# Score products of a pooled attention: one product per head on half of the array's rows, in two banks, in place of pairs of heads with zeros

## The chip, the cores and the metric

One Trainium2 chip, one core. The metric is the device time of one execution in microseconds (us), as the median of several runs. All tensors come from and go to the chip's main memory.

## The reference

Three layers follow each other, for 4 batches x 576 positions = 2304 tokens and 512 channels (8 heads x 64):

```python
k_p = k.reshape(B, H, 72, 8, 64).mean(axis=3)      # 576 keys pooled to 72
v_p = v.reshape(B, H, 72, 8, 64).mean(axis=3)
scores = scale * np.matmul(q, k_p.transpose(0, 1, 3, 2))
scores = scores - np.max(scores, axis=-1, keepdims=True)
attn = np.exp(scores); attn = attn / (np.sum(attn, axis=-1, keepdims=True) + 1e-09)
x = np.matmul(attn, v_p)                           # to (2304, 512)
x = (sigmoid(x @ w_gate) * (x @ w_val)) @ w_out    # 512 -> 1536 -> 512
h = x @ w_in                                       # 512 -> 2048
out = (h * tanh(softplus(h))) @ w2_out             # 2048 -> 512
```

The weights arrive as 64-bit floats and are converted on the chip.

## The kernel before

**Stages.** Tokens are worked on in tiles of 128 (T = 0 to 17). Attention for tiles 0 to 3 runs first; the rest of it is spread through the first three passes of the gated layer (blocks j = 0, 1, 2 of 512 tokens, twelve f each). A pass computes, for each f, `part(pg, ...)` and `part(pv, ...)` (12 products of 512 columns each) and then `emit_out` for the f before. After each of the three comes a `slot`, and a slot runs the words of one section of a schedule written out by hand (`START`, sections parted by `|`). The last 768 tokens of the gated layer and the whole second layer follow after about 340 us and are not touched.

**Order.** Every engine works its instructions strictly in the order in which the words issue them; waits come from the data and from the reuse of buffers. The words that matter: `mT.g` scores of tile T, group g (`att_scores`), `MT.g` the minimum over keys on VectorE (`att_max`; scores carry a minus sign), `XT.g` exp and sum on ScalarE, four heads one by one (`att_exp`; with `:v` partly on VectorE), `NT` the division (`att_norm`), `tT.g` transposes on TensorE, `cT.g` their copy out, `pT.g` or `OT` the products with v. Tiles from 8 on turn the weights by DMA in place of `t`. `A`, `B`, `C`, `G` are steps of weight conversion and splitting. The words around tiles 6 and 7:

```
| | m6.0 C:a M6.0 m6.1 A M6.1 X6.0 X6.1 G:v B:d C:a N6:v | A B:v C:a m7.0 M7.0 X7.0
| t6.0 c6.0:a B:e G:p Q8 | m7.1 M7.1 X7.1 t6.1 c6.1:a B:a N7:v | Q9
| t7.0 c7.0:a t7.1 c7.1:a G:v L2.0 L2.1 | O6 O7 o6 o7 | d m8.0 M8.0 m8.1 M8.1
```

Tile 4 has `m4.0` and `m4.1` in slots some 10 us apart, tile 7 in slots 6.5 us apart; elsewhere the two follow each other with no other TensorE work between.

**Scores.** `q_t[T]` holds q turned, 128 rows = two heads of 64 channels, for four pairs of heads. `kb` holds the pooled keys of a pair as 128 x 144: the even head's 72 columns have zeros in the lower 64 rows, the odd head's in the upper 64. So one product of 128 x 128 weights (q) with 144 columns (`kb`) gives the scores of both heads. Group g covers pairs 2g and 2g + 1, that is heads 4g to 4g + 3, in one bank. A float32 product shows as two records (load of weights and product) in the trace. Tiles 4 and 13 hold tokens of two batches, so each product is done in two parts of 64 tokens.

**Banks.** Scores, transposes and products with v of tiles from 4 on share the tag `at`, two buffers of 128 x 512 float32, taken in turn; a new tile waits until its buffer's last reader is done. q has two buffers as well.

Of the kernel before, what the change touches and what calls it, by code (L numbers as in the profile page):

```python
# [57 lines left out]
def tile_pooled_attention_moe_mish(  # L58
# [12 lines left out]
    nc = tc.nc  # L71
    NT, DM = out.shape
    B, _, NPAIR, S = kt.shape
    SP = S // POOL
    D = DM // (2 * NPAIR)
# [48 lines left out]
    with tc.manual_schedule():  # L124
# [90 lines left out]
        with ExitStack() as actx:  # L215
# [67 lines left out]
            kb = [pt_pool.tile([128, NPAIR, 2 * SP], F32, name=f"kb{i}") for i in range(2)]  # L283
# [95 lines left out]
            def segs(t0, n):  # L379
                done = 0  # L380
                while done < n:
                    b, s = divmod(t0 + done, S)
                    m = min(n - done, S - s)
                    yield done, m, b
                    done += m

            q_t, e_t, mx_t, sm_t, pt_t, sc_t = {}, {}, {}, {}, {}, {}
# [6 lines left out]
            def ps_tile(tag, name):  # L394
                pool = {"mm": ps_mm, "at": ps_at}.get(tag, ps_acc)
                return pool.tile([128, 512], F32, tag=tag, name=name)

            def att_scores(T, g, tag="at"):
                if g == 0:
                    e_t[T] = pt_pool.tile([128, 8, SP], F32, tag="e", name="e", bufs=2)  # L400
                    mx_t[T] = pt_pool.tile([128, 8, 1], F32, tag="mx", name="mx", bufs=2)
                    sm_t[T] = pt_pool.tile([128, 8, 1], F32, tag="sm", name="sm", bufs=2)
                ps = ps_tile(tag, "sc")
                for pp in range(2):
                    for t0, n, b in segs(128 * T, 128):
                        nc.tensor.matmul(
                            ps[t0 : t0 + n, 144 * pp : 144 * pp + 144],
                            q_t[T][:, 2 * g + pp, t0 : t0 + n],
                            kb[b % 2][:, 2 * g + pp, :],
                            start=True,  # L410
                            stop=True,
                        )
                sc_t[T, g] = ps[:, 0:288].rearrange("p (h k) -> p h k", h=4)

            def att_max(T, g):
                mx = mx_t[T][:, 4 * g : 4 * g + 4, :]
                nc.vector.tensor_reduce(out=mx, in_=sc_t[T, g], axis=AX.X, op=ALU.min)  # L417

            def att_exp(T, g, eng=None):
                s = sc_t.pop((T, g))  # L420
                if eng is nc.vector:
                    e, h = e_t[T], slice(4 * g, 4 * g + 4)
                    mx = mx_t[T][:, h, :].to_broadcast([128, 4, SP])
                    eng.tensor_sub(out=e[:, h, :], in0=mx, in1=s)
                    nc.scalar.activation(out=e[:, h, :], in_=e[:, h, :], func=AF.Exp)
                    eng.reduce_sum(out=sm_t[T][:, h, :], in_=e[:, h, :], axis=AX.X)
                    return
                for h in range(4):
                    nc.scalar.activation(  # L429
                        out=e_t[T][:, 4 * g + h, :],  # L430
                        in_=s[:, h, :],
                        func=AF.Exp,
                        scale=-1.0,
                        bias=mx_t[T][:, 4 * g + h, :],
                        accum_out=sm_t[T][:, 4 * g + h, :],
                    )

            def att_norm(T, eng):
# [164 lines left out]
            with tc.tile_pool(name="pst", bufs=1, reuse_waits="tile") as pst:  # L603
# [6 lines left out]
                    out=shift,  # L610
# [73 lines left out]
                def run(word):  # L684
# [11 lines left out]
                    elif op == "V":  # L696
                        att_values(*a, eng)
                    elif op == "m":
                        att_scores(*a, sc_tag[a[0]] if first else "at")
                    elif op == "M":  # L700
                        att_max(*a)
                    elif op == "X":
                        att_exp(*a, eng)
                    elif op == "I":
                        first_loads[a[0]](eng or nc.sync)
# [165 lines left out]
            for j, (o, n) in enumerate(blocks[:-1]):  # L871
# [26 lines left out]
                for f in range(NF):  # L898
# [11 lines left out]
                    if pv is None:  # L910
# [3 lines left out]
                        out=sg, in0=sg, scalar=1.0, in1=pv[:, :n], op0=ALU.add, op1=ALU.mult  # L914
# [71 lines left out]
            for f in range(NF):  # L986
# [52 lines left out]
                g = x1c[:, 2048 + 768 * (f % 2) : 2816 + 768 * (f % 2)].rearrange("p (a n) -> p a n", a=2)  # L1039
# [82 lines left out]
        with ExitStack() as bctx:  # L1122
# [56 lines left out]
            for p in range(NPR):  # L1179
                o = 2 * NG * p  # L1180
                for i in range(NFP):
                    n = NFP * p + i
# [144 lines left out]
```

## Time and profile before

| | us |
|---|---|
| median of 3 runs (lowest, highest) | 874.67 (874.61, 877.69) |
| the profiled execution's own time | 876.79 |
| its span in the trace | 874.7 |
| TensorE busy | 864.3 (99%) |
| VectorE / ScalarE / GpSimd busy | 618.4 / 440.2 / 98.8 |

Times of the trace count from the start of the span. PE is TensorE's products, PEld its loads of weights, DVE VectorE, ACT ScalarE, POOL GpSimd, SP the queue that issues DMAs. Records of products overlap, since each includes its way through the array; the distance between starts tells how long a product holds the array.

### The profile page before, as it was taken

The page shows a single profiled execution, that of the slowest core. Times are in us where ns is not written, and L with a number is a line of the kernel's source. Part 1 is how long each engine was busy: PE and PEld are TensorE (multiplying, and loading weights), DVE is VectorE, ACT ScalarE, POOL GpSimd, SP SyncE. Part 2 cuts the span into 40 slices and gives each one's busy share as a digit, 9 for nine tenths or more (in the row PEclk, how much of TensorE's full clock was granted, in tenths as well). Part 3 has the DMA queues.
Part 4 walks back from the last instruction along what each step waited for, and adds up shares of the span by engine and source line. Part 5 has one row for each costly group of instructions (what it writes and reads, how often), then busy time and mean ns, then how long its engine had stood idle before and what let it go on. Part 6 is the DMA issues. An engine that isn't in the chain of part 4 may idle for free.

```text
span 874.7 us, 12861 instructions
## 1 busy us (share of the span) xinstructions
PE 864.3 (99%) x4628; PEld 768.9 (88%) x4628; DVE 618.4 (71%) x1174; ACT 440.2 (50%) x1052; POOL 98.8 (11%) x110
## 2 busy tenths in 40 slices
PE   8999999999999999999999999999999999999998
PEld 7877888888878888999999999998999988999986
DVE  6879864776755754778898977767677757777632
ACT  6655663554546644534544554445454454445431
POOL 3566430120120000000100000000000000000000
PEclk9999999999999999999999999999999999999999
DMA  7688645998878877155555811202112111110011
GB/s 270 224 295 273 231 154 198 283 266 255 259 184 267 268 212 251 61 217 195 216 197 182 302 53 49 85 25 96 61 49 65 65 40 61 62 47 25 1 37 36
DMA packets 68347, 133.77 MB, mean 153 GB/s; under 512 B 27196, under 2 KB 32060, under 8 KB 68284
## 3 DMA queue, kind: packets, MB, share of 16 engines
q1 hardware_dynamic: 66988, 130.70, 46.0%
q10 hardware_dynamic: 1296, 2.26, 0.7%
q8 instruction: 36, 0.59, 0.3%
q14 instruction: 27, 0.22, 0.1%
HBM read 99.50 MB, written 28.20 MB: 146 GB/s over the span
## 4 chain that ended last, share of the span: by engine, by line
PE 89%; DMA 5%; ACT 3%; DVE 2%; POOL 1%; issue 1%; SPq 0%; POOLq 0%; ACTq 0%; DVEq 0%
PE acc L1156 23%; PE p L122 7%; PE p L120 7%; PE p L121 7%; PE acc L120 4%; PE acc L121 4%; PE acc L122 4%; PE q L120 3%; PE q L122 3%; PE q L121 3%; PE pg L566 3%; PE pv L566 3%; PE pg L567 3%; PE pv L567 3%; PE pg L570 3%; PE pv L570 3%
## 5 line engine op out<-in xcount | busy, mean ns | idle before, releaser
L1156 PE MATMUL acc<-w,g 128*128 128x512 f32 x864 | 201.1, 390 | 0.0
L1156 PEld LDWEIGHTS acc<-w,g 128*128 128x128 f32 x864 | 161.8, 188 | 32.7
L122 PE MATMUL p<-top,w2s 128*128 128x384 f32 x216 | 72.5, 336 | 0.0
L120 PE MATMUL p<-top,w2s 128*128 128x384 f32 x216 | 72.4, 335 | 0.0
L121 PE MATMUL p<-top,w2s 128*128 128x384 f32 x216 | 72.3, 335 | 0.0
L242 ACT ACTIVATE cv<-raw 128x512 f32<-128x512 f32 x66 | 44.9, 681 | 39.8 <-DMA raw<-w2i 14.3
L256 DVE SCALAR_TENSOR_TENSOR cv<-raw,cv 128x512 uint32<-128x512 uint32 x68 | 57.2, 841 | 2.3
L918 ACT CAST gh<-sg 128x512 fp32r<-128x512 f32 x36 | 22.3, 621 | 69.7 <-DVE sg L913 69.7
L120 PE MATMUL acc<-gh,wo 128*128 128x512 f32 x144 | 57.4, 398 | 0.0
L121 PE MATMUL acc<-gl,wo 128*128 128x512 f32 x144 | 56.4, 392 | 0.6 <-DVE gl L766 0.6
L122 PE MATMUL acc<-gh,wo 128*128 128x512 f32 x144 | 56.1, 390 | 0.0
L1150 DVE TENSOR_TENSOR g<-g,g 128x384 fp32r<-128x384 f32 x48 | 26.2, 557 | 31.0 <-ACT g L1146 30.7
L251 DVE TENSOR_SCALAR cv<-cv 128x512 uint32<-128x512 uint32 x68 | 37.2, 546 | 13.1 <-ACT cv L242 13.0
L429 ACT ACTIVATE e<-sc,mx 128x72 f32<-128x72 f32 x140 | 42.5, 326 | 7.2 <-DVE mx L417 7.1
L120 PEld LDWEIGHTS p<-top,w2s 128*128 128x128 f32 x216 | 40.6, 188 | 1.0
L121 PEld LDWEIGHTS p<-top,w2s 128*128 128x128 f32 x216 | 40.5, 188 | 1.0
L122 PEld LDWEIGHTS p<-top,w2s 128*128 128x128 f32 x216 | 40.5, 188 | 0.0
L120 PE MATMUL p<-x1c,w2s 128*128 128x384 f32 x120 | 40.1, 334 | 0.0
L121 PE MATMUL p<-x1c,w2s 128*128 128x384 f32 x120 | 40.1, 334 | 0.0
L122 PE MATMUL p<-x1c,w2s 128*128 128x384 f32 x120 | 40.1, 334 | 0.0
L1212 ACT ACTIVATE g<-g 128x384 f32<-128x384 f32 x24 | 12.6, 527 | 52.4 <-DVE g L1205 52.4
L1146 ACT CAST g<-g 128x384 fp32r<-128x384 f32 x48 | 23.8, 512 | 28.8 <-PE acc L1156 28.8
(261 smaller groups left out, 2153.1 us busy)
## 6 DMA issues: line engine op xcount, KB each, us to landing
wo<-wod SPq DMA_DIRECT2D x39, 512.0 KB
ws<-w2d SPq DMA_DIRECT2D x24, 512.0 KB
raw<-w2i SPq DMA_DIRECT2D x16, 512.0 KB
raw<-w2o SPq DMA_DIRECT2D x16, 512.0 KB
raw<-wv SPq DMA_DIRECT2D x12, 512.0 KB
raw<-wo SPq DMA_DIRECT2D x12, 512.0 KB
wod<-wo SPq DMA_DIRECT2D x12, 512.0 KB
wsd<-ss SPq DMA_DIRECT2D x12, 512.0 KB
```

What stands on the lines that cost most here:

```text
L120: nc.tensor.matmul(ps, wt[:, 0, cols], xh, start=start, stop=False)
L121: nc.tensor.matmul(ps, wt[:, 0, cols], xl, start=False, stop=False)
L122: nc.tensor.matmul(ps, wt[:, 1, cols], xh, start=False, stop=stop)
L242: eng.activation(out=f32(c), in_=hi, func=AF.Prelu, scale=BIAS, alpha=-(2.0**32))
L251: nc.vector.tensor_scalar(out=c, in0=c, scalar1=3, scalar2=None, op0=ALU.logical_shift_left)
L256: nc.vector.scalar_tensor_tensor(out=c, in0=lo, scalar=29, in1=c, op0=ALU.logical_shift_right, op1=ALU.bitwise_or)
L429: nc.scalar.activation(out=e_t[T][:, 4 * g + h, :], in_=s[:, h, :], func=AF.Exp, scale=-1.0, bias=mx_t[T][:, 4 * g + h, :], accum_out=sm_t ...
L566: nc.tensor.matmul(ps[:, c0:c1], w, xh[:, k, c0:c1], start=(k == 0), stop=False)
L567: nc.tensor.matmul(ps[:, c0:c1], w, xl[:, k, c0:c1], start=False, stop=False)
L570: nc.tensor.matmul(ps[:, c0:c1], w, xh[:, k, c0:c1], start=False, stop=(k == KD - 1))
L1150: nc.vector.tensor_sub(out=g[:, 1, :], in0=src, in1=f32(g[:, 0, :]))
L1156: nc.tensor.matmul(acc[t][0], g[:, a, c], w[:, b, :], start=(f == 0 and first), stop=(f == NF2 - 1 and last),)
```

## The change

For tiles from 4 on, `att_scores` with g = 0 takes both buffers of `at` and issues one product per head: the 64 rows of its channels (upper half for even heads, lower half for odd ones), 72 columns of `kb` without the zeros; even heads go to the first bank, odd heads to the second, by turns. With g = 1 it does nothing. `att_max` and `att_exp` of group 0 then cover the even heads, those of group 1 the odd ones. The schedule's words stay.

```diff
+            ROWS = 4
+            def heads(T, g):
+                return slice(g, 8, 2) if T >= ROWS else slice(4 * g, 4 * g + 4)
...
             def att_scores(T, g, tag="at"):
...
+                if T >= ROWS:
+                    if g:
+                        return
+                    ps = [ps_tile(tag, "sc") for _ in range(2)]
+                    for t0, n, b in segs(128 * T, 128):
+                        for h in range(8):
+                            r, c = slice(D * (h % 2), D * (h % 2) + D), SP * (h // 2)
+                            nc.tensor.matmul(
+                                ps[h % 2][t0 : t0 + n, c : c + SP],
+                                q_t[T][r, h // 2, t0 : t0 + n],
+                                kb[b % 2][r, h // 2, SP * (h % 2) : SP * (h % 2) + SP],
+                                start=True,
+                                stop=True,
+                            )
+                    for i in range(2):
+                        sc_t[T, i] = ps[i][:, 0:288].rearrange("p (h k) -> p h k", h=4)
+                    return
...
             def att_max(T, g):
-                mx = mx_t[T][:, 4 * g : 4 * g + 4, :]
+                mx = mx_t[T][:, heads(T, g), :]
...
             def att_exp(T, g, eng=None):
...
-                for h in range(4):
+                for h, i in enumerate(range(8)[heads(T, g)]):
                     nc.scalar.activation(
-                        out=e_t[T][:, 4 * g + h, :],
+                        out=e_t[T][:, i, :],
...
```

## Rows read from the trace of the kernel before

**Rows 1.** The page: busy time of the engines, and the chain that ended last.
```profile
PE 864.3 (99%) x4628; PEld 768.9 (88%) x4628; DVE 618.4 (71%) x1174; ACT 440.2 (50%) x1052; POOL 98.8 (11%) x110
...
PE 89%; DMA 5%; ACT 3%; DVE 2%; POOL 1%; issue 1%; SPq 0%; POOLq 0%; ACTq 0%; DVEq 0%
```

**Rows 2.** Windows: length, busy us (instructions) of PE, PEld, DVE, ACT, POOL; clock; DMA share, GB/s.
```profile
57.50:311.00 253.50, 252.06 (x1350) 207.32 (x1347) 177.24 (x324) 137.82 (x387) 57.18 (x65) 1.00 0.79 241
...
311.00:874.00 563.00, 559.85 (x2908) 515.76 (x2906) 397.90 (x773) 265.33 (x542) 12.20 (x12) 1.00 0.30 102
```

**Rows 3.** Line of the score products, 55 to 320 us: count, lowest/median/highest ns, forms.
```profile
L406 PEld LDWEIGHTS sc<-kb,q x128: 132/190/190, 57.2 to 309.5; 128*128 128x128 f32 x96, 128*64 128x64 f32 x32
L406 PE MATMUL sc<-kb,q x128: 285/286/337, 57.2 to 309.6; 128*128 128x144 f32 x96, 128*64 128x144 f32 x32
```

**Rows 4.** Timeline of PE at tile 12: start us, length us, instruction.
```profile
213.55 1.14 PE L406 MATMUL sc<-kb,q 128*128 128x144 f32 x8
214.44 0.49 PE L566 MATMUL pv<-x,wv 128*128 128x512 f32 x1
214.76 0.40 PE L567 MATMUL pv<-x,wv 128*128 128x512 f32 x1
```

**Rows 5.** Timeline of PE at tile 13, products on half of the columns.
```profile
232.53 0.61 PE L570 MATMUL pg<-x,wg 128*128 128x512 f32 x2
233.08 1.20 PE L406 MATMUL sc<-kb,q 128*64 128x144 f32 x16
234.21 0.50 PE L566 MATMUL pv<-x,wv 128*128 128x512 f32 x1
234.55 0.40 PE L567 MATMUL pv<-x,wv 128*128 128x512 f32 x1
```

**Rows 6.** Timeline of PE at the first pooled values: full rows, 64 rows, full rows.
```profile
16.27 0.42 PE L341 MATMUL vh<-vp,shift 128*72 128x64 f32 x4
16.62 0.34 PE L338 MATMUL vh<-vp,shift 64*72 64x64 f32 x2
16.89 0.34 PE L341 MATMUL vh<-vp,shift 128*72 128x64 f32 x2
```

**Rows 7.** Groups by form, weight loads of line 338: busy us, mean ns.
```profile
L338 PEld LDWEIGHTS vh<-vp,shift 128*72 128x72 f32 x6 | 0.6, 145 | 0.0
L338 PEld LDWEIGHTS vh<-vp,shift 64*72 64x72 f32 x2 | 0.2, 138 | 0.1
```

**Rows 8.** Timeline of DVE, ACT and PE around tiles 6 and 7.
```profile
117.75 0.46 DVE L417 TENSOR_REDUCE mx<-sc 128x4 f32<-128x288 f32 x1 [2.30 <-PE sc L406]
...
120.58 0.33 ACT L429 ACTIVATE e<-sc,mx 128x72 f32<-128x72 f32 x1
120.78 0.21 ACT L429 ACTIVATION_READ_ACCUMULATOR e<-sc,mx 128x1 f32 x1
120.78 0.65 PE L406 MATMUL sc<-kb,q 128*128 128x144 f32 x4
...
124.05 0.60 PE L452 MATMUL tr<-ident,e 128*72 128x128 f32 x4
...
125.14 0.32 ACT L429 ACTIVATE e<-sc,mx 128x72 f32<-128x72 f32 x1 [2.02 <-DVE mx L417]
...
126.25 0.21 ACT L429 ACTIVATION_READ_ACCUMULATOR e<-sc,mx 128x1 f32 x1
...
127.25 0.65 PE L406 MATMUL sc<-kb,q 128*128 128x144 f32 x4
```

**Rows 9.** Timeline at tile 4: a wait for gl, the division and the first transposes.
```profile
58.96 0.50 PE L121 MATMUL acc<-gl,wo 128*128 128x512 f32 x1 [0.61 <-DVE gl L766]
...
75.35 0.76 DVE L443 TENSOR_TENSOR e<-e,sm 128x576 f32<-128x576 f32 x1
...
76.25 0.60 PE L452 MATMUL tr<-ident,e 128*72 128x128 f32 x4
```

**Rows 10.** Timeline of PE behind tile 14's scores.
```profile
260.80 0.50 PE L566 MATMUL pv<-xh,wv 128*128 128x512 f32 x1 [0.63 <-DVE sg L913]
```

More of the change, by code (lines that the diff above doesn't have):

```diff
@@ L421, in att_exp @@
                 if eng is nc.vector:
-                    e, h = e_t[T], slice(4 * g, 4 * g + 4)
+                    e, h = e_t[T], heads(T, g)
                     mx = mx_t[T][:, h, :].to_broadcast([128, 4, SP])
@@ L433, in att_exp @@
                         scale=-1.0,
-                        bias=mx_t[T][:, 4 * g + h, :],
-                        accum_out=sm_t[T][:, 4 * g + h, :],
+                        bias=mx_t[T][:, i, :],
+                        accum_out=sm_t[T][:, i, :],
                     )
```

## The prediction, made before the change was run

> **What bounds the kernel now.** I read the page's engine shares and chain first [rows 1]: TensorE (PE) is busy for 864.3 of 874.7 us and carries 89% of the chain that ended last. Then the stretch that holds all changed work, 57.5 to 311 us, and what follows it [rows 2]: PE is busy for 252.06 of 253.50 us and 559.85 of 563.00 us, at granted clock 1.00 (2.4 GHz), while VectorE (DVE) has 177 of 253.5 and ScalarE (ACT) 138. So a us that PE gains or loses there reaches the end, except where PE itself waits for another engine; I then looked for those places. "Busy" hides pitch, so the costs are read from starts in the timeline.
>
> **What the score products cost now.** Tiles 4 to 17 have 128 records [rows 3]: each float32 product is two records. 12 tiles have 8 records of 128 x 128 weights; tiles 4 and 13 cross a batch and have 16 of 64 columns.
> - A whole tile (tile 12): from the first score product at 213.55 to the second of the next part at 214.76 is 1.21 us; less the 0.23 that one such 512-column product takes (232.53 and its neighbours, x2 in [rows 5], start 0.226 apart), 0.98 us for eight, 0.1225 each [rows 4]. There is no gap before it.
> - Tile 13: its 16 records on halves of the columns run from 233.08 to 234.21, and the next part's second product starts at 234.55: 1.47 us less 0.23 [rows 5]. Sixteen took hardly longer than eight, so two halves work at once, eight steps of 0.1225 = 0.98. The rest is the change between full and half array: the first half product starts at 233.08 and not at 232.53 + 2 x 0.226 = 232.98 (+0.09), its load lies open (+0.05), and the way back costs +0.09 and an open full load, +0.11. That makes 0.98 + 0.35 = 1.33 us.
> - Products on 64 of the rows occur once before [rows 6]: four full ones begin at 16.27, 0.065 apart (0.42 less one record of 0.23, over three), so the last ends its turn at 16.53, the half-row pair starts at 16.62 (+0.09) and holds PE until 16.89, 0.27 where two cost 0.13. So half rows pay the same change.
>
> **The change, part by part.** Per whole tile it puts 16 records in place of 8, each with 72 moved columns in place of 144 and 128 weight columns as before. Moving costs 0.1225 / 2 = 0.061. The load does not halve: a 64-row load of 72 columns has a record of 138 ns, a 128-row one 145 [rows 7]; loads go by columns. The 128-column record is 190 [rows 3], 45 ns more than at 72 columns, and 72-column loads with only 64 columns to move come every 0.065 [rows 6], so a 128-column load needs 0.065 + 0.045 = 0.110 us.
>
> *Not shown before:* whether the upper and lower 64 rows work at once. Column halves do, loads included [rows 5]; I take that for the row halves. Then a pair of heads steps at the longer of load and move, 0.110: change 0.09 + eight steps 0.88 + last move 0.06 + change back 0.09 + open load 0.11 = 1.23 us, against 0.98: **+0.25 us a tile**. The lower bound is loads that hide, steps of 0.061: 0.09 + 0.11 + 0.49 + 0.09 + 0.11 = 0.89, -0.09 a tile. The upper is no overlap: 0.09 + 16 x 0.11 + 0.26 = 2.11, +1.13. I stay at the middle, the row nearest in kind being tile 13's.
>
> The Trainium skill, "TensorE: Matmul & The Clock Gate", section "LDWEIGHTS (loading the stationary operand)", puts a load in ns at its columns divided by 1.2, whatever its rows, which speaks against this change; by its 107 ns for 128 columns, an estimate, a tile would cost +0.23 and the sum would be 0.3 us less. The loads of [rows 7] agree that rows don't count.
>
> Which tiles pay:
> - Tiles 5 to 12 and 15 to 17, eleven: no wait of PE lies behind them that could swallow the loss. 11 x 0.255 = **+2.8**.
> - Tile 13: half columns before and after, 64-column loads that fit under 0.061 moves; the two segments follow each other, 16 x 0.061 = 0.98 as before: 0.
> - Tile 14: PE waits for DVE at 260.80 [rows 10], a delay that comes through loads of v and not through PE, so the 0.25 goes into that wait: 0. Without the cover, +0.25.
> - Tile 4: its two groups (0.49 + 0.35 = 0.84 each) become one of 1.33 at the first place. The 0.49 more there ends in PE's wait for gl at 58.96 (0.61 to 0.88) [rows 9]. The 0.84 less at 67 us takes PE sooner to the transposes of tile 4, which start at 76.25, when DVE's normalisation (75.35 + 0.76) has just ended [rows 9]; DVE comes to that by its own queue, so PE waits 0.84 longer: 0. If DVE moved too, -0.84.
>
> **The banks.** The tag "at" has two buffers. Until now group 0 takes one and group 1 the other, at its own word of the order; now group 0's word takes both and group 1's does nothing on PE. For most tiles both were long free. Not for tiles 6 and 7, whose words are m6.0 .. m6.1 .. X6.0 X6.1 | m7.0 M7.0 X7.0 | t6.0 | m7.1 M7.1 X7.1 t6.1:
> 1. M6.0 can start when the even heads are done, about 0.54 later than the 117.75 at which DVE had already been waiting for them [rows 8] (eight steps now lie before it, not four). DVE and ACT run their queues in order, so X6.0, X6.1, the cast of wg, N6, M7.0 and X7.0 all come 0.54 later.
> 2. m7.0 needs the second bank, so X6.1: its last exp starts at 120.58, is over at 120.99, now 121.53 [rows 8]. PE is there at 120.78 + 0.25 and does one head first: wait **0.4**.
> 3. t6.0 took the bank of X6.1; now it takes that of X7.0, which starts at 125.14 and whose last record ends at 126.46, now 127.0 [rows 8]. PE arrives at 124.05 + 0.25 + 0.4 + 0.75 (the whole of m7 is now ahead of it, 1.23 for 0.49) = 125.45: wait **1.6**. Queued behind it on PE are the out products and everything else; c6.0 on ACT comes late too.
> 4. t6.1 needs X7.1, which on ACT follows c6.0 and a cast; PE loses m7.1 (-0.49, at 127.25) and arrives at 130.27, X7.1 ends near 130.35: 0.1.
>
> Together **+2.1**, 0 if the queues had slack that I miss. Elsewhere M comes 0.5 later where DVE waited for it, with nothing due soon. Exps, minima and splits keep their counts and sizes, only with every second head, so I cost them at nothing; no DMA is added, and the reload of q waits for products that come no later than now.
>
> **Sum.** 2.8 + 2.1 = +4.9 us on the span of 874.7. That execution took 876.79 in all (2.1 around the span); the median run is 874.67, to which I add it: **879.6 us**. DMA has 0.79 of the time in this stretch [rows 2]; a slower PE relieves it, which may return some tenths.
>
> **Rivals.**
> - *Loads hide (not slower).* Row halves then step at 0.061. For it: loads of column halves hid behind moves in tile 13; against it: there a load of 64 columns met a move of 144, here 128 meets 72 [rows 3, 5]. Eleven tiles give -1.0, but M6.0 still comes 0.2 late and t6.0 then waits 2.2, with 0.25 around it: +1.45, 876.1 us. It decides if a pair steps under 0.09 us. The skill's page above, section "Part 3: Packing small matmuls — row/col tiling", has this rule: a pack lasts one product and about 4 ns for each further one. No run here shows it for row halves.
> - *No overlap.* If the two row halves take turns, the halving does not do what it says: 11 x 1.13 = 12.4, about 1 at tiles 13 and 14 beyond their cover, and waits of 0.9 (PE comes later, so t6.0 waits 0.7): 889 us. For it: no row shows two row halves; against it, [rows 5].
> - *No bank waits.* X7.0 early enough for t6.0: 877.5 us. Against it: DVE has no idle time before M7.0, and ACT waited 2.02 for it [rows 8].
>
> **How the numbers follow.** 0.5% (4.4 us, about what a measurement of this kernel tells from no change) puts the line at 879.0. Main case 0.66, own range 877.4 to 881.5; three fifths of it beyond the line (0.40 slower, 0.26 same). Loads hide 0.14 (same), no overlap 0.15 (slower), no bank waits 0.05 (same, but for a gain of 0.02 if tile 4 and hidden loads came together with them). Slower 0.55, same 0.43, faster 0.02. The range runs from hidden loads, 875.8, to steps half way to no overlap, 884.5.
>
> **What would show it.** In the profile after: a whole tile's score products about 1.2 us from the end of one part to the second product of the next, heads in pairs 0.11 apart; gaps of 0.09 at both ends; PE waiting for ACT at t6.0 near 126 us for over a microsecond, and at the second head of tile 7; the wait at 260.80 shorter. Pairs 0.06 apart, or single records 0.11 apart, or no gap at t6.0, would prove the sum wrong, as would PE waits at later tiles.

## The result and the profile after

The median is 881.77 us over 5 runs (880.29 to 882.79), against 875.48 us over 5 runs of the kernel before (874.61 to 878.55; two more than ahead of the prediction). The quotient of the medians is 1.0072; the ratio on record, taken from all these runs, is 1.006, 95% interval 1.0046 to 1.0075. So the changed kernel is slower, by about 0.6%; the lower end of the interval lies just under the 0.5% at which the prediction drew its line. The profiled execution took 881.09 us, its span 879.2; the predicted time was 879.6 with a range of 875.8 to 884.5.

The page of the kernel after: span, busy engines, and the shares of the chain that ended last [rows 1].

```profile
span 879.2 us, 13105 instructions
...
PE 867.3 (99%) x4756; PEld 768.8 (87%) x4756; DVE 615.7 (70%) x1174; ACT 440.0 (50%) x1052; POOL 99.3 (11%) x110
...
PE 88%; DMA 4%; DVE 4%; ACT 3%; issue 1%; SPq 0%; POOL 0%; DVEq 0%; ACTq 0%
```

PE has 128 records more and 3.0 us more of busy time; DVE's share of the chain has doubled, from 2 to 4%. The page doesn't say more than that: the cost is in pitches (the distances between the starts of products) and in a few waits, and these are seen in the timeline.

PE at tile 12 after the change, the same stretch as [rows 4]: start, length, instruction.

```profile
217.20 0.61 PE L592 MATMUL pg<-x,wg 128*128 128x512 f32 x2
217.75 1.11 PE L415 MATMUL sc<-kb,q 64*128 64x72 f32 x16
218.79 0.50 PE L588 MATMUL pv<-x,wv 128*128 128x512 f32 x1
219.13 0.39 PE L589 MATMUL pv<-x,wv 128*128 128x512 f32 x1
```

By the same count as before (217.75 to 219.13, less the 0.23 of one 512-column product, and now with the gap of 0.09 ahead), the tile costs 1.24 us; the records one by one give 1.249 against 0.990. The products behind it take a little longer to settle as well, so that from tile to tile the shift against the kernel before grows by 0.273. Within the group, single records start in pairs 6 to 7 ns apart, an even and an odd head, and the pairs follow each other after 0.167 (once) and then 0.112 us (six times), 0.843 from first to last. Nine other whole tiles show the same cost to 0.001 us; tiles 5 and 7 differ by a wait.

PE at tile 13 [rows 5], where each product is in two parts of 64 tokens.

```profile
237.46 1.03 PE L415 MATMUL sc<-kb,q 64*64 64x72 f32 x32
238.42 0.50 PE L588 MATMUL pv<-x,wv 128*128 128x512 f32 x1
238.76 0.40 PE L589 MATMUL pv<-x,wv 128*128 128x512 f32 x1
```

Thirty-two records are issued in 0.81 us, which is less than the 0.98 of two segments in turn: the second segment (other columns) begins before the first is over. The tile costs 1.167 us in place of 1.333.

Tiles 6 and 7 after the change, PE, ACT and DVE [rows 8]. In brackets stand the idle time before the instruction and what ended it.

```profile
117.63 1.11 PE L415 MATMUL sc<-kb,q 64*128 64x72 f32 x16
118.78 0.46 DVE L439 TENSOR_REDUCE mx<-sc 128x4 f32<-128x288 f32 x1 [2.85 <-PE sc L415]
121.62 1.55 PE L415 MATMUL sc<-kb,q 64*128 64x72 f32 x16
121.80 0.21 ACT L451 ACTIVATION_READ_ACCUMULATOR e<-sc,mx 128x1 f32 x1
...
126.15 0.32 ACT L451 ACTIVATE e<-sc,mx 128x72 f32<-128x72 f32 x1 [2.01 <-DVE mx L439]
127.25 0.21 ACT L451 ACTIVATION_READ_ACCUMULATOR e<-sc,mx 128x1 f32 x1
...
127.52 0.63 PE L474 MATMUL tr<-ident,e 128*72 128x128 f32 x4 [1.39 <-ACT e L451]
```

Tile 7's group lasts 1.55 where an undisturbed one lasts 1.11: after its first head it waits 0.43 us for the bank of X6.1, whose last record is the one at 121.80. Then t6.0 starts at 127.52, straight after X7.0's last record (127.25 + 0.21); PE had nothing else to do for 1.39 us by the profile's own count, and by the shift against the kernel before it lost 1.58 there.

Tile 5, PE, DVE and POOL: a wait that was not foreseen.

```profile
90.17 1.29 POOL L275 TENSOR_TENSOR wg<-cv,wg 128x512 fp32r<-128x512 f32 x1 [0.31 <-ACT wg L112]
90.18 1.83 DVE L256 SCALAR_TENSOR_TENSOR cv<-raw,cv 128x512 uint32<-128x512 uint32 x1
...
91.20 0.44 PE L415 MATMUL sc<-kb,q 64*128 64x72 f32 x2
91.93 0.41 DVE L500 TENSOR_TENSOR x<-pv,x 128x256 fp32r<-128x256 f32 x1
...
92.40 1.11 PE L415 MATMUL sc<-kb,q 64*128 64x72 f32 x14 [0.77 <-DVE x L500]
```

One head of tile 5 is issued, then the odd bank is missing until DVE has read tile 4's products with v (word l4.1, line 500) out of it. The group costs 2.445 us, 1.20 more than a whole tile. DVE's instruction ahead of that read took 1.83 us; it began 0.01 after a product of POOL and ended 0.55 after it. In the kernel before the two stood in the other order:

```profile
91.08 0.69 DVE L256 SCALAR_TENSOR_TENSOR cv<-raw,cv 128x512 uint32<-128x512 uint32 x1
91.17 1.75 POOL L275 TENSOR_TENSOR wg<-cv,wg 128x512 fp32r<-128x512 f32 x1 [0.66 <-ACT wg L112]
...
91.69 0.42 DVE L478 TENSOR_TENSOR x<-pv,x 128x256 fp32r<-128x256 f32 x1
```

There DVE's took 0.69 and POOL's was the long one. So PE came 0.92 us earlier to tile 5, and the read of the second bank 0.24 later.

Behind tile 14, where PE waited for DVE before [rows 10]: DVE's reduction that transfers of v release, in the kernel before,

```profile
256.00 0.68 DVE L373 TENSOR_REDUCE vb<-vr 72x64 f32<-72x512 f32 x1 [4.10 <-DMA vr<-vt]
```

and DVE and PE after the change:

```profile
258.23 0.68 DVE L373 TENSOR_REDUCE vb<-vr 72x64 f32<-72x512 f32 x1 [2.55 <-DMA vr<-vt]
...
262.30 0.68 DVE L935 SCALAR_TENSOR_TENSOR sg<-sg,pv 128x512 f32<-128x512 f32 x1
...
264.35 0.39 PE L588 MATMUL pv<-xh,wv 128*128 128x512 f32 x1
```

DVE's product that PE had waited for is done at 262.98, and PE, now late, comes for it only at 264.35: no wait is left.

**Where the time went.** The table subtracts the start of the same PE product in the two traces and gives the change of that shift over each stretch, for two profiles of the changed kernel (the second is a run further below). The last column gives the same for two more profiles of the kernel before, unchanged (also below): it shows what a stretch varies by without any change.

| stretch, us of before | predicted | measured | second profile | before, twice more |
|---|---|---|---|---|
| 0 to 55, no changed work | 0 | -0.50 | -0.89 | +1.79, -0.68 |
| to 117: tiles 4 and 5 | +0.25 | +0.98 | +1.42 | +1.62, +0.29 |
| to 144: tiles 6 and 7 | +2.6 | +2.54 | +2.53 | -0.01, -0.01 |
| to 233: tiles 8 to 12 | +1.3 | +1.36 | +1.37 | 0, 0 |
| to 250: tile 13 | 0 | -0.12 | -0.12 | 0, 0 |
| to 269: tile 14 and the waits behind it | 0 | -1.35 | -1.35 | -0.23, +0.32 |
| to 320: tiles 15 to 17 | +0.8 | +0.58 | +0.58 | -0.24, -0.24 |
| to the end, no changed work | 0 | +0.97 | +0.60 | +1.08, -0.11 |
| sum | +4.9 | +4.46 | +4.14 | +4.02, -0.42 |

The first and the last row vary as much from profile to profile of the kernel before, so they are not read as the change's, and the second row only where its records show a wait. Tiles 6 to 13 hardly vary: what they show is the change's.

### The profile page after: what moved, and what is told of

The parts are those of the page before. It is cut to its first block, busy times and chain, and to the rows that moved or that the text cites. A ratio compares the mean times of both kernels' runs of the same rounds, so it can differ in the third digit from the quotient of the medians.

```text
span 879.2 us, 13105 instructions
## 1 busy us (share of the span) xinstructions
PE 867.3 (99%) x4756; PEld 768.8 (87%) x4756; DVE 615.7 (70%) x1174; ACT 440.0 (50%) x1052; POOL 99.3 (11%) x110
## 4 chain that ended last, share of the span: by engine, by line
PE 88%; DMA 4%; DVE 4%; ACT 3%; issue 1%; SPq 0%; POOL 0%; DVEq 0%; ACTq 0%
PE acc L1178 22%; PE p L122 7%; PE p L120 7%; PE p L121 7%; PE acc L120 4%; PE acc L121 4%; PE acc L122 4%; PE pv L588 3%; PE q L121 3%; PE q L120 3%; PE q L122 3%; PE pv L589 3%; PE pv L592 3%; PE pg L589 3%; PE pg L588 3%; PE pg L592 3%
```

## Experiments

The theory: row halves do work at once, the load of 128 columns sets a step of 0.11 us, the change of form and the open loads around it eat what the shorter moves could give, and two waits for banks come on top. Rivals to it: the step is set by the products themselves, or tile 7's waits are DVE and ACT being late by themselves, whatever the banks. The edits below are against the changed kernel where nothing else is said.

**The change from tile 8 on only** (`e1_tiles8`):

```diff
-            ROWS = 4
+            ROWS = 8
```

> Only tiles 8 to 17 take the new form; tiles 4 to 7 stay as before. Theory (loads and the change between full and half rows cost 0.27 us a whole tile; the rest came from waits for the second bank at tiles 5 and 7): each of tiles 8 to 12 starts 0.27 later than the one ahead of it, as with the full change, no new wait lies before them, and of 1.3 us so gathered most is swallowed by the waits near 260 us that the kernel before has; at the end +0.3 to +1.2 us on before (span 875 to 876), 3.5 us under the full change. Rival (no bank waits, the whole loss is in the products): 10 of 13 paying tiles remain, so the loss stays above 3 us (span over 877.5).

877.84 us against 876.22, ratio 1.0036 (1.0015 to 1.0057); span 875.8, end of PE's work 1.12 later than in the profile of before. Tiles 8 to 12 pay 0.273 each again, tile 11 a wait on top. Between 256 and 269 us the shift falls from +1.12 to -0.06, although PE was only 1.1 late there: the waits of before swallow what has built up, up to their own length. A new wait showed at tile 11, DVE and PE:

```profile
195.40 1.28 DVE L516 TENSOR_TENSOR xl<-pv,xh 128x512 fp32r<-128x512 f32 x2
...
196.31 1.53 PE L415 MATMUL sc<-kb,q 64*128 64x72 f32 x16
```

The group of 1.53 has a hole of 0.42 before its second bank is read out; the next experiment shows it there too (0.44). So taking both banks at the first word can make waits at other tiles, where PE runs closer to DVE.

**Tile 6's transposes ahead of tile 7's scores** (`e2_order`), in the schedule:

```diff
-... | A B:v C:a m7.0 M7.0 X7.0 | t6.0 c6.0:a A B:e G:p Q8 | m7.1 M7.1 X7.1 t6.1
-c6.1:a B:a N7:v | ...
+... | A B:v C:a | t6.0 c6.0:a t6.1 c6.1:a A B:e G:p Q8 | m7.0 M7.0 X7.0 m7.1
+M7.1 X7.1 B:a N7:v | ...
```

(The words quoted ahead of the prediction leave out the `A` between `c6.0:a` and `B:e`.)

> The full change, with the words of tile 6's transposes and copies put ahead of tile 7's scores, which move into the slot of m7.1. Theory (t6.0 waited for X7.0 only because it took the bank that tile 7's even scores held, and m7.0 for X6.1): both waits go, tile 8's scores start 0.9 to 1.3 us later than before in place of 3.1, and the span is about 2 us under the full change, 877.2. Rival (VectorE and ScalarE are late there by themselves, and PE would wait in any order): PE waits as long at the transposes, tile 8 stays 3 us late, span 879.

878.98 us, ratio 1.0045 (1.0028 to 1.0063) against the same runs of before; span 876.6. PE's records at tiles 6 and 7:

```profile
117.28 1.12 PE L415 MATMUL sc<-kb,q 64*128 64x72 f32 x16
124.16 1.04 PE L474 MATMUL tr<-ident,e 128*72 128x128 f32 x8
```

All eight transposes start together, without a wait, and tile 7's group lasts 0.844 from first to last start like the others. The shift at 144 us is +0.86 in place of +3.02. The waits belong to the banks, as predicted; the rival falls.

**Twice the columns moved** (`e3_wide`): each half-row product moves 144 columns, those of both heads of its pair. The odd heads come in descending order, so that the surplus columns are written over.

```diff
-                        for h in range(8):
+                        for i in range(8):
+                            h = i if i % 2 == 0 else 8 - i
...
-                                ps[h % 2][t0 : t0 + n, c : c + SP],
+                                ps[h % 2][t0 : t0 + n, c : c + 2 * SP],
...
-                                kb[b % 2][r, h // 2, SP * (h % 2) : SP * (h % 2) + SP],
+                                kb[b % 2][r, h // 2, :],
...
```

> Each half-row product moves 144 columns of kb (its own head's 72 and 72 zeros, which a later product of the same bank overwrites); loads and order otherwise as in the change. Theory (the load of 128 weight columns, 0.112, sets the step): doubling the move lengthens the step only to 0.1225, a whole tile's group from 0.84 to about 0.93 us from first to last start, and tiles 4 and 13, whose loads are of 64 columns, lengthen most. Rival (the moved columns, or a cost in proportion to them, set the step): it doubles to 0.22, the group to 1.7 us, 0.8 us more for each of 12 tiles.

One execution: 882.95 us, span 881.0. PE at a whole tile:

```profile
181.54 1.25 PE L416 MATMUL sc<-kb,q 64*128 64x144 f32 x16
```

0.968 us from first to last start, pairs 0.1225 apart, the step that 144 columns set before. Moving twice as much costs 0.0105 a step: with 72 columns it was the load of 0.112 that set it, and the moves of 0.061 lay under it. In turns the step would have been twice as long.

**All even heads, then all odd heads** (`e4_noturns`):

```diff
-                        for h in range(8):
+                        for h in (0, 2, 4, 6, 1, 3, 5, 7):
```

> The same products, even heads first and then odd heads, in place of by turns. Theory (the two row halves overlap only as far as PE looks ahead in its queue, which is a few records): the halves run one after the other, 16 steps of 0.112, a group of about 1.7 us in place of 0.84, +0.85 for each of 12 tiles, span some 9 us over the full change. Rival (PE starts the odd heads out of order whatever the distance): 0.85 as in the change, span 879.

One execution: 886.73 us, span 884.8. PE at a whole tile:

```profile
182.32 1.62 PE L415 MATMUL sc<-kb,q 64*128 64x72 f32 x16
```

1.344 from first to last start, which neither theory gave. The single records explain it: eight even ones 0.112 apart to 183.152, while the odd ones begin at 182.823, with the fifth even one, and run on alone to 183.66. So the other half is started ahead of its turn, but only from about four records away; issuing by turns is what makes the halves work at once throughout, and it is worth 0.50 us a tile.

**The change of form alone** (`e5_halfcols`): the kernel before, with the products of every tile from 4 on cut into two parts of 64 tokens, as tiles 4 and 13 have it anyway.

```diff
+                parts = list(segs(128 * T, 128))
+                if T >= 4:
+                    parts = [(t + u, 64, b) for t, n, b in parts for u in range(0, n, 64)]
...
-                    for t0, n, b in segs(128 * T, 128):
+                    for t0, n, b in parts:
```

> The kernel before, with the scores of every tile from 4 on in two parts of 64 tokens (as tiles 13 and 4 have it), pairs with zeros and banks as before: the change of array form alone, without row halves. Theory (the change of form costs what tile 13 shows, 0.35 us a group, and two column halves work at once): each whole tile costs 1.33 in place of 0.98, tiles 7 and 5 with two groups or one alike 0.35 a group; tiles 8 to 12 start 0.35 later each. Rival (the cost belongs to row halves, tile 13 was special): 0.98 to 1.1 a tile.

One execution: 880.81 us, span 878.9. PE at a whole tile:

```profile
179.99 1.20 PE L409 MATMUL sc<-kb,q 128*64 128x144 f32 x16
```

1.333 us against 0.990, and 0.353 a tile in the shift. The products and the steps are the same; the 0.35 is the price of going to half the array and back, the figure read from tile 13 [rows 5].

**Quarters** (`e6_quarters`): if the load sets the step, halve the load. Each half-row product is cut into two parts of 64 tokens, so four quarters of the array take turns.

```diff
-                    for t0, n, b in segs(128 * T, 128):
-                        for h in range(8):
+                    half = [(t + u, 64, b) for t, n, b in segs(128 * T, 128) for u in range(0, n, 64)]
+                    for h2 in range(0, 8, 2):
+                        for t0, n, b in half:
+                            for h in (h2, h2 + 1):
...
```

> The change with each product cut into two parts of 64 tokens, by turns over the four quarters of the array (two row halves, two column halves): loads of 64 columns, moves of 72. Theory (the load sets the step in the change; quarters work at once): four quarters step together every 0.0615, a group lasts about 0.45 us from first to last start in place of 0.84, and with both changes of form a whole tile costs 0.85 to 0.9 against 0.98 before and 1.25 in the change. The waits for banks at tiles 5 to 7 stay (about 2.3), so the span is 4 us under the full change less what the waits near 260 us then don't swallow: 875.5 to 877. Rival (loads share one path, or PE looks ahead too little): steps of 0.11 or more for four, 1.25 a tile, span 879.

877.48 us against 875.93, ratio 1.0025 (1.0013 to 1.0037); span 877.5, that of the slowest of its seven runs (the span of their median is 875.5). PE at tile 4, at tile 5 and at a whole tile:

```profile
58.92 0.62 PE L417 MATMUL sc<-kb,q 64*64 64x72 f32 x4 [0.79 <-ACT kb L298]
...
92.65 0.34 PE L417 MATMUL sc<-kb,q 64*64 64x72 f32 x2
93.86 0.72 PE L417 MATMUL sc<-kb,q 64*64 64x72 f32 x30 [0.87 <-DVE x L502]
...
180.45 0.73 PE L417 MATMUL sc<-kb,q 64*64 64x72 f32 x32
```

Thirty-two records now need 0.508 us, steps of 0.0625: close to the 0.061 that the moves need. A whole tile costs 0.867, which is 0.12 less than before the change; the products behind it take longer to settle, and in the shift 0.07 is left. The waits for banks stayed (1.2 at tile 5, and at tile 7). The span of the profile was above what was expected, that of the median run was not; the profile has a wait at tile 4, where the group took 1.93 us. That one is not for a bank but for pooled keys (`kb`) that ACT writes, of which the change needs those of all four pairs at the first place. It varies: in the next experiment, with the same products at tile 4, the group took 0.56 us.

**Quarters in the other order** (`e7_quarters_order`): the edits of the second and the sixth experiment together.

> Quarters, with tile 6's transposes put ahead of tile 7's scores. Theory: quarters without the waits at tile 7, so 0.1 us gained a tile and half a us at tiles 4 and 13: span 873 to 875, ratio to before 0.998 to 1.0. Rival (the waits belong to VectorE and ScalarE): as the quarters alone, 875.5 to 877.

875.50 us against 875.93, ratio 0.9997 (0.9983 to 1.0011); span 872.9. At 320 us PE stood 3.55 us ahead of the profile of before, of which 0.84 came from before 55 us; behind 470 us it lost 1.75 of that again, most of it waiting for weights from memory. At tile 5, where the sixth experiment waited for 1.2 us, PE did not wait, though both banks are taken at once here too; DVE and POOL there, and the weights:

```profile
89.91 0.69 DVE L256 SCALAR_TENSOR_TENSOR cv<-raw,cv 128x512 uint32<-128x512 uint32 x1
89.94 1.81 POOL L275 TENSOR_TENSOR wg<-cv,wg 128x512 fp32r<-128x512 f32 x1 [0.34 <-ACT wg L112]
90.52 0.42 DVE L502 TENSOR_TENSOR x<-pv,x 128x256 fp32r<-128x256 f32 x1
90.96 0.76 PE L417 MATMUL sc<-kb,q 64*64 64x72 f32 x32
...
488.22 0.41 PE L120 MATMUL ac<-gs,wo 128*128 128x384 f32 x1 [0.84 <-DMA wo<-wod]
```

DVE's product began 0.03 ahead of POOL's and took 0.69, and l4.1 (at 90.52) was over at 90.94, just before tile 5.

**The kernel before, twice more** (`e8_before_a`, `e9_before_b`), unchanged. They ask whether the waits near 260 us belong to the kernel or to one execution, and how far the ends of the table vary.

> The kernel before, profiled once more. Seven changed kernels, early and late, all came through 257 to 266 us without the waits of 1.3 us that the first profile of before shows there. Theory: those waits belong to that one execution (its transfers of v landed late) and not to the kernel, so a second profile has none or shorter ones, its span is 873 to 874, and the difference of spans understated the change by a us or more. Rival (my first reading: the waits belong to the kernel, and a later PE swallows them): they are there again, 1.3 us in all, span 874.7.

> The kernel before, a third profile: as the second, to see how much the stretches 0 to 60 us and 478 to 491 us differ from run to run by themselves. Theory: by up to half a us ahead of 60 us and up to 1 us near 485 us, where PE waits for weights of the last product from memory in some runs.

880.61 us (span 878.7) and 876.32 us (span 874.2). The first, though unchanged, took as long as the second profile of the changed kernel (880.74, below): single executions can't tell the two kernels apart, the ratios rest on several. That first of them at tile 5 (POOL, DVE, PE) and behind tile 14:

```profile
93.54 1.29 POOL L275 TENSOR_TENSOR wg<-cv,wg 128x512 fp32r<-128x512 f32 x1 [0.24 <-ACT wg L112]
93.62 1.75 DVE L256 SCALAR_TENSOR_TENSOR cv<-raw,cv 128x512 uint32<-128x512 uint32 x1
95.30 0.41 DVE L478 TENSOR_TENSOR x<-pv,x 128x256 fp32r<-128x256 f32 x1
...
95.76 0.76 PE L406 MATMUL sc<-kb,q 128*128 128x144 f32 x4 [0.63 <-DVE x L478]
...
263.98 0.50 PE L566 MATMUL pv<-xh,wv 128*128 128x512 f32 x1 [0.57 <-DVE sg L913]
```

and the second behind tile 14:

```profile
260.71 0.50 PE L566 MATMUL pv<-xh,wv 128*128 128x512 f32 x1 [0.59 <-DVE sg L913]
```

The wait behind tile 14 is there each time, so it is the kernel's; that it was only one execution's falls. At tile 5 the first of these two shows the new wait without the change, POOL's product having begun just ahead of DVE's: that order is a matter of some tenths of a us. Against the first profile of before, these stood +1.79 and -0.68 us at 55 us, and +1.08 and -0.11 came between 470 us and the end: what the first and the last row of the table show for the change is within that.

**Quarters, other order, and the second bank of tile 5 read out earlier** (`e10_best`):

```diff
-... C:a G:v l4.0 A B:a l4.1 C:a B:a C:a A | m5.0 A C:a A
+... C:a G:v l4.0 l4.1 A B:a C:a B:a C:a A | m5.0 A C:a A
```

> Quarters of the array by turns, tile 6's transposes ahead of tile 7's scores, and the last read of tile 4's second bank moved ahead of two conversion steps on VectorE, so that tile 5 finds both banks free. Theory: 0.12 to 0.14 us gained at each of 12 tiles and half a us at tiles 4 and 13 and no new wait, 2 to 3 us under the kernel before in the stretch of the change; ratio 0.996 to 0.999. Rival (what PE gains ahead of 120 us is lost again to VectorE, as at tile 4 in the change): ratio 0.999 to 1.001.

876.35 us against 876.25, ratio 1.0 (0.9985 to 1.0015); span 874.5. PE at tile 5 and the one wait behind it:

```profile
92.13 0.73 PE L417 MATMUL sc<-kb,q 64*64 64x72 f32 x32
102.33 0.50 PE L590 MATMUL pv<-xh,wv 128*128 128x512 f32 x1 [1.04 <-DVE sg L937]
```

The wait at tile 5 is gone and comes back 10 us later, for DVE. The expected gain did not come; the ratio is the rival's, which had PE lose to DVE again what it gains here. Of all versions none is measurably faster than the kernel before.

**The changed kernel again** (`e11_after`), unchanged.

> The full change, profiled once more. Theory: what the change itself causes comes again to the hundredth (1.25 us a whole tile, 1.17 at tile 13, waits of 0.4 and 1.6 at tile 7), the wait for the second bank at tile 5 comes again but of another length (0.3 to 1.3 us), since it hangs on when VectorE's last read of the bank ahead comes. Rival: the wait at tile 5 was that run's alone, and is gone.

880.74 us, span 878.8: the last column of the table. Whole tiles 1.249 and tile 13 1.167 as in the first profile, the wait at tile 5 and both at tile 7 equal to 0.01 us.

**Both moves of words, without quarters** (`e12_banks`): the changed kernel with the edits of the second and the tenth experiment.

> The full change with both orders mended: tile 6's transposes ahead of tile 7's scores, and l4.1, the last read of the second bank ahead of tile 5's scores, moved ahead of two conversion steps on VectorE. Theory (tile 5's wait of 1.2 us hangs on the place of l4.1 in VectorE's queue): tile 5's group is 0.84 us from first to last start as the others, no wait within, and what is left of the change is the products alone, 11 tiles of 0.27; the span is 0.5 to 1.2 us under the full change with only tile 7's order mended, 875.5 to 876.2. Rival (VectorE is the floor of the stretch up to 120 us, and PE only waits elsewhere for it): the wait at tile 5 goes, but as much comes back at a later place before 120 us, and the span stays at 876.6 or above.

878.56 us against 875.28, ratio 1.0037 (1.0021 to 1.0052); span 876.8. PE and DVE around tile 5:

```profile
91.16 1.11 PE L415 MATMUL sc<-kb,q 64*128 64x72 f32 x16
...
100.47 0.64 DVE L935 SCALAR_TENSOR_TENSOR sg<-sg,pv 128x512 f32<-128x512 f32 x1
...
101.16 0.50 PE L588 MATMUL pv<-xh,wv 128*128 128x512 f32 x1 [0.51 <-DVE sg L935]
```

No wait at tile 5 any more; the next one is at 101.16, straight after DVE's `sg`. The span is the rival's again (876.6 or above). At 117 us the shift is +0.10, with the wait at tile 5 kept (second experiment) it was +0.14. Of the 1.20 saved at tile 5, 0.78 comes back at 101 us; some 0.3 had been lost ahead of it, at tile 4's wait for pooled keys, whose group took 1.11 us in place of 0.81. DVE has little slack here: windows of the kernel before give it 39.65 busy us of the 43.50 from 57.5 to 101, 91%, against 71% of the whole span.

## Why the prediction was right where it was, and wrong where not

The time lay 2.2 us above the forecast and inside its range; the ratio's interval, applied to the 875.5 of the median before, gives +4.0 to +6.6 against a forecast of +4.9. By points:

- *Row halves at once, step 0.110 set by the load:* right. Pairs 6 to 7 ns apart, steps of 0.112; with twice the columns moved 0.1225, with half the columns loaded 0.0625. The Trainium skill, "TensorE: Matmul & The Clock Gate", section "LDWEIGHTS (loading the stationary operand)", gives a load by its columns alone, by its formula 107 ns for 128 (an estimate); the step of 0.112 is 5 ns longer and does not halve with the rows, which agrees. The Trainium skill's same page, section "Part 3: Packing small matmuls — row/col tiling" counts a pack as one product and about 4 ns for each further one. The pairs' 6 to 7 ns come near that, but the rival built on it, hidden loads with steps of 0.061, fell: here the load outlasts the move. With quarters, where it does not, the steps were 0.0625.
- *Price of a whole tile, +0.25:* +0.273. The change of form was the assumed one: 0.35 by itself in the fifth experiment.
- *Banks, +2.1:* right in place and cause, +2.0 in size (0.43 within tile 7 for 0.4, 1.58 at t6.0 for 1.6, and no wait at t6.1 for 0.1). The rival without bank waits falls with it.
- *"For most tiles both were long free":* wrong for tile 5, whose odd heads waited 1.20 us for l4.1. I had gone through the holders of the banks only at tiles 6 and 7. The banks alone don't make this wait: PE waited at tile 5 in all eight profiles in which POOL's product began ahead of DVE's and l4.1 stood in its old place, also in two without row halves at tile 5 (the fifth experiment, and the kernel before at 95.76), and in none of the four in which DVE's began first, also not with both banks taken at once (seventh). POOL began first in eight of nine profiles with row halves at tile 5 and in two of five without; whether the change brings that about stays open. The same step had tile 4's gain of 0.84 taken back at the transposes of 76.25; there PE waited only 0.40 by the profile (75.25), and the rest of its lead was lost here. Both are one error: PE was taken to run free of DVE in this stretch but for those two places, while up to about 101 us DVE takes back much of what PE gains, as the tenth and the last experiment show. Net, the stretch cost +0.98 and +1.42 for the predicted +0.25; some 0.5 and 0.9 of that is the early start below 55 us, which is lost as well, and against the kernel before PE stood 0.48 and 0.53 late at 117 us. Since the kernel before by itself gave +1.62 and +0.29 here, how much of this row is the change's is not shown.
- *Tile 13, 0:* -0.17 by its own records, -0.12 in the shift. I let the two segments of it follow each other; they overlap.
- *Tile 14, 0:* the mechanism was right in part, the size wrong. I let only this tile's own 0.25 go into the wait for DVE. But PE's whole lateness of 4.5 us stood against it, and the wait depends on transfers of v: the reduction that they release [DMA vr<-vt] began at 256.00 before and 258.23 after, 2.2 later with PE 4.5 later. So all the waits from 257 to 269 us went, 1.35 us and the tile's 0.27, 1.62 in all. What counts is PE's lateness less that of the reduction. In all thirteen profiles after the first, the stretch gives back that difference to 0.03 us, up to 1.62: in the first experiment 1.18 (PE 1.12 late, the reduction 0.05 early), in the last 0.82 (2.31 and 1.50 late), in the first repetition of the kernel before only 0.23 (3.41 and 3.19 late). In the seventh and tenth PE was early or hardly late (-1.92, +0.28), but the reduction was earlier still (-3.07, -1.11), and 1.17 and 1.39 went. What sets when these transfers land stays open.
- *Tiles 15 to 17, +0.8:* right. Each paid its 0.273, +0.82 together. The table's +0.58 is 0.24 less because the first profile of before waits for ACT at 286.48; the two later profiles of the same kernel don't, and fall by the same 0.24, so that is no effect of the change.
- *"DMA may return some tenths":* not seen; the ends of the table vary by more.

The two largest terms, the eleven tiles and the banks, were met in mechanism and in size. That the sum was met as well is partly luck: the misses, +0.7 to +1.2 at tiles 4 and 5, -1.35 behind tile 14 and -0.1 at tile 13, happen to offset each other, and the stretches without changed work add from -0.3 to +0.5.

## What to carry to other kernels

Halving the columns that a product moves gains nothing once the load of the stationary operand, which goes by its own columns, sets the step (here 0.112 us against 0.061 for the move); and the change between the full array and a part of it costs some 0.35 us per group here, to be paid before any gain. An edit that takes two buffers at once where the order took them one after the other has to be checked against the last reader of each buffer at every place, above all where the engine that reads is itself the bound. A late engine swallows the waits that lie ahead of it, up to their full length, by as much as it is later than the work it waits for: all its lateness counts and not only its last step's, but where that work is late with it, nothing is swallowed. And a stretch that differs between two traces should be looked up in a second trace of the unchanged kernel before it is called the change's.

## What was unexpected of the hardware

- PE starts a product for an idle half of the rows ahead of the queue's order, from about four records away: the odd heads of the fourth experiment began with the fifth even record. So the order ahead of the prediction, every engine strictly in the order of the words, doesn't hold to the letter for PE's products.
- Halves of rows and of columns combine: with four quarters by turns, four records start within 20 ns and the next four 0.113 us later once, then 0.0625 on average.
- Of an instruction of DVE (line 256) and one of POOL (line 275) that overlap, the one that starts second lasts as if it waited for the first: at 90.18 DVE's took 1.83 us in place of 0.69, at 92.74, 0.03 behind DVE's, POOL's took 1.81 in place of 1.29. The Trainium skill, "SBUF — State Buffer", section "SBUF: two separate sides", states this as an exclusive lock of a shared pair of ports that whichever starts first holds for its whole instruction, among others for one of DVE with two inputs in SBUF against one of GpSimd that reads there. The rows agree but for some 0.14 us: DVE's ended 0.55 behind POOL's and alone takes 0.69. Here a start 0.1 us to one or the other side goes with whether tile 5 waits; no run kept the two apart.
